# Two attentions in one program: loads and GpSimd work put at other steps, with the same arithmetic

## The chip, the core and the metric

The kernel runs on one core of a Trainium2 chip. The metric is the device time of one execution in microseconds, lower is better. Five engines work from instruction streams of their own and meet at semaphores: TensorE (PE in the profile; PEld is its weight load), VectorE (DVE), ScalarE (ACT), GpSimd (POOL) and SyncE (SP). SP computes nothing here: it issues DMA transfers, in the order of its stream, and an instruction of any stream that has to wait holds up all that stand behind it in that stream.

## The reference

Two attentions over 2048 positions of 576 features, 32 heads of 18 features each, in float32. A looks at 8 keys per query, 2 positions apart, backwards; B at all 2048 keys. Their outputs stand beside each other.

```python
# A: sliding, dilated window          S, D, H, Dh = 2048, 576, 32, 18; scale = Dh ** -0.5
q, k, v = split_heads(x @ wqkv)
idx = pos[:, None] - arange(8) * 2                 # idx < 0 is masked
logits = einsum("bhsd,bhswd->bhsw", q, k[idx]) * scale
o = einsum("bhsw,bhswd->bhsd", softmax(logits), v[idx])
a = merge_heads(o) @ wo
# B: every key
scores = einsum("bhqd,bhkd->bhqk", q, k) * scale
b = merge_heads(einsum("bhqk,bhkd->bhqd", softmax(scores), v)) @ wo
return concatenate([a, b], axis=-1)
```

## The kernel before

The program has a projection stage and a main loop.

**Projection stage** (up to 415 us). PE makes queries, keys and values, first B's and then A's. Nearly every float32 operand is split into a high and a low part, and a product is three matmuls. `stream` runs the later products two at a time on the two halves of PE's rows, and puts between them the first *maxima* of B: a matmul `bank<-ks,qs` (L159), whose 128x512 result DVE reduces to a maximum per row (L166). The stage goes by *slots*, one for each product: `at(n, f)` puts f at the n-th slot from now. The projections are written to DRAM (`dqk` for B, L468; `da` for A, L652) and read back as rows of heads. B's heads come in 8 groups g of four, and a set `qs, ks` holds one group. Three sets rotate. `second_rows`, called at a slot, makes set 1 and asks for its 12 loads (`stack_loads(1)`, L143 and L144, 288 KB each), one per slot, from POOL's own DMA queue. SP has the other transfers of the stage: the inputs of A (`raw<-xa`, `more<-xa`, L363), the weights (`raw<-wa`), and the write-backs. ACT makes the high parts and empties the banks, POOL most of the low parts (`xlo`, `olo`, `alo`).

**Main loop.** 512 *steps*, 64 per group: four blocks of 512 queries by 16 key tiles kt. A step is four score matmuls (`bank<-qs,ks`, L229), three or four maxima for later blocks (L159, L166), four exponentials on ACT (L235), and the eight matmuls `po<-e,v` (L701) of the step before, which weigh the values. Some steps also hold 27 matmuls more, a product of A's output with its output weights. Beside this goes an *agenda*: `plan` and `later` put small functions at a step number, and `due()` emits those of a step at its end. An engine keeps to the order of emission, not to the step: where nothing holds it up SP runs ahead, and POOL falls behind when it has much to do.

**The end of a block of B** (`finish`, L706). It comes at a step s that is a multiple of 16. ACT copies `po` to `o`. Then the agenda has: `den<-o`, the 4 denominators' rows out of `o` (s+1, SP, L733); a reciprocal on DVE (s+8, L734); `drec<-den` (s+9, SP) and `rec<-drec` (s+13, SP), which spread the reciprocals over partitions; *the division*, three POOL instructions `o<-o,rec`, `n<-o`, `n<-o,n` (s+18 to s+20, L737 to L739); and the store `do<-n` (s+26, SP). `rec` and `n` have one buffer each.

**A inside the main loop** (`local`). A's attention is done in 8 *parts* j of 256 positions. Part j starts at step 10 + 54j. Relative to that step: `fetch` brings queries (0), keys (1) and values (28) from `dpart`; POOL multiplies and adds for the logits `lg` (`match`, 5 to 25, nine times); DVE takes the maximum over the 8 keys in three halvings (`most`, 31 to 33, `am`, L859); POOL subtracts it (33), ACT exponentiates (35), DVE sums in three halvings (`total`, 36 to 38, `as`, L859) and inverts (`inverses`, 38 and 39, L875); POOL scales `lg` (`share`, 39, L878) and weighs the values (`weighted`, 39 to 59). The halvings are called *the trees* below. `dpart` is a copy of `da` in another layout, made before by three DRAM-to-DRAM transfers of SP (`arrange`, `dpart<-da`, L822), from 24 steps ahead of the part, and not before step 14 of the group:

```python
at = A_FROM + GAP * j - 24
at = max(at, STEPS * (at // STEPS) + 14) - A_FROM - GAP * j
```

That gives the first of the three at steps 3 (set apart for j = 0), 40, 94, 148, 206, 270, 310 and 364.

**Output weights.** `load_wo` loads a chunk of `woa` or `wob` to a tile `y` (four buffers, shared with outputs) and three steps later POOL splits it (L104, L105). A's five chunks come at steps 28, 32, ... 44, B's at 404, 408, ... 420. A's are first used at step 88, B's at 488.

Of the kernel before, what the change touches and what calls it, by code (L numbers as in the profile page):

```python
# [22 lines left out]
NG = H // 4  # L23
# [10 lines left out]
STEPS = NB * NT  # L34
# [9 lines left out]
GAP = 54  # L44

A_FROM = 10


def ap(t, *dims):

    return bass.AP(tensor=t.tensor, offset=t.offset, ap=[list(t.ap[0])] + [list(d) for d in dims])


def rows(t, *dims):

    return bass.AP(tensor=t.tensor, offset=t.offset, ap=[list(d) for d in dims])
# [3 lines left out]
def two_attentions(ctx: ExitStack, tc, xa, wa, woa, xb, wb, wob, out):  # L60
# [5 lines left out]
    nc = tc.nc  # L66
# [42 lines left out]
    step = 0  # L109
# [4 lines left out]
    def plan(start, pieces):  # L114
        for n, f in pieces:
            agenda[start + n].append(f)
# [8 lines left out]
    def make_set(pool, i):  # L125
        qs = pool.tile([128, NB, 2, 512], F32R, name=f"qs{i}")
        ks = pool.tile([128, 2, S], F32R, name=f"ks{i}")
        sets.append((qs, ks))

    def ones_loads(i):  # L130
        ks = sets[i][1].bitcast(F32)
        return [lambda r=r: load(ap(ks[64 * r + 54 : 64 * r + 56], (128, 2 * NT), (1, 128)), ap(ones, (0, 2 * NT), (1, 128)))
                for r in range(2)]
# [108 lines left out]
    def load_v(g):  # L242
        vs[g] = (work if g % 2 else maxes).tile([128, NT, 4 * 19], F32, name="v", bufs=1)
        load(vs[g], dv[g])
# [85 lines left out]
    def do_all(fs):  # L330
        for f in fs:
            f()
# [6 lines left out]
    with (tc.tile_pool(name="x", bufs=1, side="right") as xp,  # L339
# [104 lines left out]
        if True:  # L444
# [9 lines left out]
            chunks = [[(0, 0, 128)], [(0, 128, third - 128), (D, 0, 256 - third)], [(D, 256 - third, 128)]]  # L454
# [67 lines left out]
            def at(n, *fs):  # L522

                while len(todo) <= n:
                    todo.append([])
                todo[n].extend(fs)
# [24 lines left out]
            def store_values(h, v2):  # L551
                for i, v in enumerate(v2):
                    load(dv[4 * h + 2 * i : 4 * h + 2 * i + 2].rearrange("g p t c -> p g (t c)"),
                         v.rearrange("p g t h d -> p g (t h d)"))
# [22 lines left out]
            def second_rows():  # L577

                store_values(1, v2)
                kept.close()  # L580
                stack1 = ctx.enter_context(tc.tile_pool(name="stack1", bufs=1, reuse_waits="tile"))
                make_set(stack1, 1)
                do_all(ones_loads(1))
                zeros = xp.tile([128, 512], F32, name="ohi", bufs=4)
                nc.gpsimd.memset(zeros[:108, : 16 * HALO], 0.0)
                load(rows(da[0], ((HALO + S) * 16, 108), (HALO + S, 16), (1, HALO)), zeros[:108, : 16 * HALO])
                for i, f in enumerate(stack_loads(1, issue=nc.gpsimd.dma_start)):
                    at(5 + i, f)
                load_v(0)

            wa_room = ExitStack()
# [48 lines left out]
            for k in range(2, 14):  # L640
                n = 46 if k == 2 else 36 + 4 * k
# [7 lines left out]
            def leave_a(c, b, n, ps):  # L649
                o = xp.tile([128, 512], F32, name="ohi", bufs=4)  # L650
                nc.scalar.activation(o[:n], ps, AF.Copy)  # L651
                load(da[128 * c : 128 * c + n, HALO + 512 * b : HALO + 512 * b + 512], o[:n])  # L652
# [23 lines left out]
            for c, b in order:  # L676
                n = min(128, 3 * D - 128 * c)
                work_list.append(((b % 2, ws[c][0], xas[b][0], slice(0, n), every),
                                  lambda ps, n=n: ps[:n], lambda ps, c=c, b=b, n=n: leave_a(c, b, n, ps)))
# [12 lines left out]
        step = 0  # L692
# [13 lines left out]
    def finish(g, b):  # L706
        o = work.tile([128, 512], F32, name="o", bufs=2)
        if g == NG - 1 and b == NB - 1:
            return closing(b, o, work.tile([128, 512], F32, name="rec", bufs=1))
        nc.scalar.activation(o, po, AF.Copy)  # L710
        den = work.tile([128, 16], F32, name="den", bufs=2)
        rec = work.tile([128, 512], F32, name="rec", bufs=1)
        parts = []

        def room():
            if g == NG - 1 and b == 0:

                parts[:] = [ap(work.tile([128, 4, 128], F32R, name=f"at{i}", bufs=1), (1, 512)) for i in range(2)]
            else:
                n = work.tile([128, 2, 512], F32R, name="n", bufs=1)  # L720
                parts[:] = n[:, 0], n[:, 1], n
            return parts

        if g == NG - 1 and b > 0:
            return shortly(b, o, rec, *room()[:2])

        def store():
            if g < NG - 1:
                load(do[:, g, :, 512 * b : 512 * b + 512].rearrange("i p n -> p i n"), parts[2].bitcast(F32))
            else:  # L730
                plan(step, full(b, parts))

        for at, f in ((1, lambda: load(den, o[DH:128:32])),  # L733
                      (8, lambda: nc.vector.reciprocal(den, den)),  # L734
                      (9, lambda: load(drec[g, b].rearrange("i (p n) -> (i p) n", n=16), den)),
                      (13, lambda: load(rec, rows(drec[g, b], (512, 4), (0, 32), (1, 512)))),
                      (18, lambda: nc.gpsimd.tensor_mul(o, o, rec)),  # L737
                      (19, lambda: nc.gpsimd.tensor_copy(room()[0], o)),
                      (20, lambda: nc.gpsimd.tensor_sub(parts[1], o, parts[0])),  # L739
                      (26, store)):  # L740
            later(at, f)

    def shortly(b, o, rec, hi, lo):
# [45 lines left out]
    wo = {}  # L789

    producing = set()

    def load_wo(k, src, *pieces):

        raw = work.tile([128, D], F32, name="y", bufs=4)
        n = 0
        if len(pieces) == 4:
            nc.gpsimd.memset(raw, 0.0)
            n = 128
        for at, c0, m in pieces:  # L800
            load(raw[at : at + m], src[c0 : c0 + m])
            n = max(n, at + m)
        if k == "a":
            hi = work.tile([128, D], F32R, name="wohi", bufs=5)
            lo = work.tile([128, D], F32R, name="wolo", bufs=5)
        else:

            c = len(wo.get(k, []))
            hi, lo = (ap(t[:, 0, 0, :] if len(t.shape) == 4 else t[:, 0, :], (1, NB * 1024))[:, D * c : D * c + D]
                      for t in sets[(NG - 3) % 3])  # L810
        wo.setdefault(k, []).append((hi, lo))
        later(3, lambda: split_on(nc.gpsimd, hi[:n], lo[:n], raw[:n]))


    def local(j):
# [4 lines left out]
        def arrange(n):  # L820
            wide = (HALO if n else 0) + SUB
            load(rows(dparts[j][n][0, 0], (wide, D), (D * wide, 4), (1, wide)),  # L822
                 rows(da[D * n, HALO + p0 + SUB - wide :], (HALO + S, D), (SUB, 4), (1, wide)))
# [95 lines left out]
        def sums_of_a(h):  # L919
# [3 lines left out]
            if h == 0:  # L923
# [6 lines left out]
        pieces = [(0, lambda: fetch("q")), (1, lambda: fetch("k")), (28, lambda: fetch("v")), (33, lower),  # L930
                  (35, exponents), (39, share), (60, upper), (61, rest), (64, lambda: put(0)), (66, lambda: put(1))]

        pieces[:0] = [(at, lambda f=f, n=n: f(n)) for f, ats in ((most, (31, 32, 33)), (total, (36, 37, 38)),
                                                                (inverses, (38, 39))) for n, at in enumerate(ats)]
        for c in range(DH // 2):
            pieces.append((5 + 5 * c // 2, lambda c=c: match(c)))
            pieces.append((39 + 5 * c // 2, lambda c=c: weighted(c)))
        at = A_FROM + GAP * j - 24

        at = max(at, STEPS * (at // STEPS) + 14) - A_FROM - GAP * j  # L940
        for n in range(3):
            pieces.append((at + n if j else n - 7, lambda n=n: arrange(n)))
        for n, (at, ends) in enumerate(((70, (78, 80)), (81, (87, 89)))):
            pieces.append((at, lambda n=n: get(n)))
            for h in range(2):
                pieces.append((ends[h], lambda h=h: finished(h)))
                producing.add(A_FROM + GAP * j + ends[h] + 1)
            pieces.append((ends[1] + 6, lambda n=n: load(out[p0 + 128 * n : p0 + 128 * n + 128, :D], ys["a", j, n])))
# [132 lines left out]
        waiting.append(lambda: sum_of(y, t, h, olds[b]))  # L1081
        sums[t, b, h] = (y,)

    for k, src, start, chunks in (
        ("a", woa, 28, [[(0, 128 * c, 128)] for c in range(4)] + [[(64 * r, 512, 64) for r in range(2)]]),
        ("b", wob, STEPS * (NG - 2) + 20,
         [[(0, 126 * c, 126)] for c in range(4)] + [[(32 * i, 504 + DH * i, DH) for i in range(4)]]),
    ):
        plan(start, [(4 * c, lambda k=k, src=src, ch=ch: load_wo(k, src, *ch)) for c, ch in enumerate(chunks)])
    for j in range(NJ):  # L1090
        plan(A_FROM + GAP * j, local(j))
    for g in range(1, NG):
# [16 lines left out]
    total = early + rest  # L1109
# [22 lines left out]
    while step < ALL:  # L1132
        n, kt = divmod(step, NT)
        g, b = divmod(n, NB)
# [50 lines left out]
```

## Time and profile before

| | us |
|---|---|
| median of 3 runs (lowest, highest) | 1646.38 (1645.86, 1647.27) |
| the profiled execution | 1646.54 |
| its span, first to last instruction | 1644.8 |
| PE busy in the span (share) | 1633.1 (99%) |
| DVE busy | 1397.0 (85%) |
| ACT busy | 1221.9 (74%) |
| POOL busy | 959.2 (58%) |

The profiled execution has 1.74 us outside its span and lies 0.16 us above the median. The page says of itself that matmuls are pipelined and that their ends are modelled: a busy PE need not be a PE at full rate. So the loss of a step is read from the starts of matmuls. A row of the timeline gives start, duration, engine, line, operation, out<-in, shape and count; in brackets stands the idle time of the engine before it and what ended it. "SPq" is SP issuing a DMA: the time is that of the issue, not of the transfer. The rows of windows give, for each stretch, every engine's busy time with its number of instructions, the granted clock, the busy share of the DMA engines and their GB/s.

### The profile page before, as it was taken

The numbers are of one execution on the slowest core, as the hardware profiler recorded it, in microseconds if no ns is written. First come the engines' busy times: TensorE is split into PE (matmuls) and PEld (weight loads), VectorE is DVE, ScalarE is ACT, GpSimd is POOL, SyncE is SP. The second block draws the span as 40 slices with busy tenths as digits, with TensorE's granted clock in tenths as the row PEclk, the third lists the DMA queues.
The fourth block names the chain that finished last, engine by engine and source line by source line (L and its number), as shares of the span: only waits on it lengthen the run. The fifth ranks groups of instructions, "written<-read, shape, count | busy, mean of one in ns | idle before, by whom it ended". The sixth has DMA issues, their size and how long they took to land.

```text
span 1644.8 us, 33745 instructions
## 1 busy us (share of the span) xinstructions
PE 1633.1 (99%) x12906; PEld 935.0 (57%) x12906; DVE 1397.0 (85%) x2366; ACT 1221.9 (74%) x2419; POOL 959.2 (58%) x792
## 2 busy tenths in 40 slices
PE   9999999999999999999999999999999999999998
PEld 7999879998433444444344344344344344445676
DVE  5199989999899989889889899889899989888533
ACT  6314432111899998998998998998998998998554
POOL 2306642210195995994994994994995996940000
PEclk9999999999999999999999999999999999999999
DMA  8837955522515347157139325716526132033201
GB/s 252 238 113 204 257 165 140 134 87 90 95 48 100 98 120 135 54 139 143 53 93 161 82 77 130 147 65 122 134 79 117 65 107 78 21 114 123 101 37 59
DMA packets 188353, 188.22 MB, mean 114 GB/s; under 512 B 118384, under 2 KB 132208, under 8 KB 186464
## 3 DMA queue, kind: packets, MB, share of 16 engines
q1 hardware_dynamic: 183328, 174.53, 40.9%
q0 software_dynamic: 4032, 10.63, 3.0%
q8 instruction: 101, 1.65, 0.4%
q10 hardware_dynamic: 832, 0.92, 0.2%
q14 instruction: 60, 0.49, 0.1%
HBM read 113.16 MB, written 88.12 MB: 122 GB/s over the span
## 4 chain that ended last, share of the span: by engine, by line
PE 96%; DMA 2%; DVE 1%; ACT 0%; POOL 0%; issue 0%; SPq 0%; ACTq 0%; POOLq 0%; DVEq 0%
PE po L701 30%; PE bank L229 25%; PE bank L322 16%; PE bank L159 13%; PE bank L1010 7%; PE bank L259 5%; DMA den<-o 1%; DVE mx L166 1%; DMA dqk<-ohi 0%; POOL xlo L370 0%; DMA first<-xb 0%; DVE am L859 0%; SPq L363 0%; DMA out<-y 0%; PE bank L985 0%
## 5 line engine op out<-in xcount | busy, mean ns | idle before, releaser
L166 DVE TENSOR_REDUCE mx<-bank 128x1 f32<-128x512 f32 x2048 | 1288.1, 683 | 144.6 <-PE bank L159 115.8
L235 ACT ACTIVATE e<-bank 128x512 f32<-128x512 f32 x2048 | 1060.2, 613 | 94.3 <-PE bank L229 51.0
L159 PE MATMUL bank<-ks,qs 54*128 54x512 f32 x2048 | 752.7, 423 | 2.1 <-DVE mx L166 2.0
L229 PEld LDWEIGHTS bank<-qs,ks 56*128 56x128 f32 x2048 | 331.1, 186 | 454.1 <-ACT e L235 423.6
L229 PE MATMUL bank<-qs,ks 56*128 56x512 f32 x2048 | 582.0, 425 | 0.0
L701 PE MATMUL po<-e,v 128*19 128x512 f32 x4096 | 538.1, 599 | 0.0
L159 PEld LDWEIGHTS bank<-ks,qs 54*128 54x128 f32 x2048 | 340.8, 185 | 15.6 <-DVE mx L166 7.6
L841 POOL TENSOR_TENSOR pr<-aq,akv 128x1024 f32<-128x1024 f32 x72 | 158.4, 2201 | 28.1 <-DMA akv<-dpart 25.6
L701 PEld LDWEIGHTS po<-e,v 128*19 128x19 f32 x4096 | 70.6, 97 | 182.1 <-issue 171.4
L884 POOL TENSOR_TENSOR pr<-lg,akv 128x1024 f32<-128x1024 f32 x72 | 158.1, 2196 | 0.6
L845 POOL TENSOR_TENSOR pr<-pr 128x1024 f32<-128x1024 f32 x64 | 152.5, 2382 | 5.0
L651 ACT ACTIVATE ohi<-bank 128x512 f32<-128x512 f32 (+1 forms) x56 | 30.5, 595 | 148.3 <-issue 116.9
L322 PE MATMUL bank<-xlo,ahi 64*128 64x512 f32 (+1 forms) x448 | 117.9, 389 | 1.4 <-POOL xlo L370 1.4
L322 PE MATMUL bank<-xhi,alo 64*128 64x512 f32 (+1 forms) x448 | 116.1, 388 | 0.0
L322 PE MATMUL bank<-xhi,ahi 64*128 64x512 f32 (+1 forms) x448 | 113.7, 388 | 1.1 <-ACT ohi L651 1.1
L885 POOL TENSOR_TENSOR pr<-pr 128x512 f32<-128x512 f32 x72 | 92.3, 1282 | 5.6
L370 POOL TENSOR_TENSOR alo<-raw,ahi 128x512 fp32r<-128x512 f32 (+1 forms) x14 | 17.6, 1254 | 121.1 <-ACT ahi L369 86.7
L463 POOL TENSOR_TENSOR olo<-olo,ohi 128x512 fp32r<-128x512 f32 x36 | 46.1, 1294 | 63.8 <-ACT ohi L462 58.4
L737 POOL TENSOR_TENSOR o<-o,rec 128x512 f32<-128x512 f32 x29 | 37.2, 1284 | 64.3 <-DMA rec<-drec 35.4
L322 PEld LDWEIGHTS bank<-xlo,ahi 64*128 64x128 f32 (+1 forms) x448 | 67.2, 182 | 7.6 <-POOL xlo L370 2.5
L322 PEld LDWEIGHTS bank<-xhi,alo 64*128 64x128 f32 (+1 forms) x448 | 65.8, 182 | 5.3
L322 PEld LDWEIGHTS bank<-xhi,ahi 64*128 64x128 f32 (+1 forms) x448 | 63.8, 181 | 7.2 <-ACT ohi L651 1.5
(197 smaller groups left out, 1790.5 us busy)
## 6 DMA issues: line engine op xcount, KB each, us to landing
do<-n SPq DMA_DIRECT2D x28, 512.0 KB
da<-ohi SPq DMA_DIRECT2D x52, 256.0 KB
dpart<-da SPq DMA_DIRECT2D x16, 702.0 KB
akv<-dpart SPq DMA_DIRECT2D x16, 702.0 KB
out<-y SPq DMA_DIRECT2D x32, 288.0 KB
qs<-dqk SPq DMA_DIRECT2D x30, 288.0 KB
ks<-dqk SPq DMA_DIRECT2D x30, 288.0 KB
at<-dao SPq DMA_DIRECT2D x64, 128.0 KB
```

Of the source, the lines that this page charges most:

```text
L159: nc.tensor.matmul(ps, qs[at, b, p, 128 * t : 128 * t + 128], ks[at, p, 512 * k : 512 * k + 512], start=True, stop=True)
L166: nc.vector.tensor_reduce(mx[:, r, p, t, k : k + 1], ps, axis=AX.X, op=ALU.max)
L229: nc.tensor.matmul(ps, ks[at, p, 128 * kt : 128 * kt + 128], qs[at, b, p], start=True, stop=True)
L235: nc.scalar.activation(e, ps, AF.Exp, scale=SCALE)
L259: nc.tensor.matmul(ps, a, b, start=c == i == 0, stop=c == 4 and i == 1)
L322: nc.tensor.matmul(ps, a, b, start=start, stop=stop)
L701: nc.tensor.matmul(po[32 * i : 32 * i + 19], vs[g][:, kt, 19 * i : 19 * i + 19], es[i], start=kt == 0, stop=kt == NT - 1)
L841: nc.gpsimd.tensor_mul(pr, ap(st["q"][:, 2 * c], (SUB, 2), (0, W), (1, SUB)), window(st["k"], c))
L845: nc.gpsimd.tensor_add(st["pr"], st["pr"], pr)
L884: nc.gpsimd.tensor_mul(at, ap(st["lg"], (0, 2), (SUB, W), (1, SUB)), window(st["v"], c))
L885: nc.gpsimd.tensor_add(at[:, :, :4], at[:, :, :4], at[:, :, 4:])
L1010: nc.tensor.matmul(ps, a, b, start=start, stop=stop)
```

## The change

It has four parts. Each engine executes the same instructions as before, and on PE, DVE and ACT they stand in the same order. What differs is the order on POOL and SP, and the waits that follow from it.

1. `arrange` starts at steps written out in a list: 3, 36, 100, 154, 186, 250, 308, 362 for j = 0 to 7.
2. The division of a block, and its store, move later by `apart` steps: the fewest for which its three steps are none of the trees' nominal steps (`most`, `total`, `inverses` of any part). It is 6 for the block that ends at step 80, 2 at 192, 8 at 240, 4 at 352, 10 at 400, and 0 for all others.
3. The chunks of `woa` are loaded at steps 2, 4, ... 10 in place of 28, 32, ... 44, and those of `wob` at 452, 456, ... 468 in place of 404, 408, ... 420.
4. The 12 loads of set 1 are asked for 10 slots later in the projection stage.

```diff
+ARRANGED = (3, 36, 100, 154, 186, 250, 308, 362)
...
                 for i, f in enumerate(stack_loads(1, issue=nc.gpsimd.dma_start)):
-                    at(5 + i, f)
+                    at(15 + i, f)
                 load_v(0)
...
+        apart = next(k for k in range(16) if not pieces_of_a.intersection(range(step + 18 + k, step + 21 + k)))
         for at, f in ((1, lambda: load(den, o[DH:128:32])),
                       (8, lambda: nc.vector.reciprocal(den, den)),
                       (9, lambda: load(drec[g, b].rearrange("i (p n) -> (i p) n", n=16), den)),
                       (13, lambda: load(rec, rows(drec[g, b], (512, 4), (0, 32), (1, 512)))),
-                      (18, lambda: nc.gpsimd.tensor_mul(o, o, rec)),
-                      (19, lambda: nc.gpsimd.tensor_copy(room()[0], o)),
-                      (20, lambda: nc.gpsimd.tensor_sub(parts[1], o, parts[0])),
-                      (26, store)):
+                      (18 + apart, lambda: nc.gpsimd.tensor_mul(o, o, rec)),
+                      (19 + apart, lambda: nc.gpsimd.tensor_copy(room()[0], o)),
+                      (20 + apart, lambda: nc.gpsimd.tensor_sub(parts[1], o, parts[0])),
+                      (26 + apart, store)):
             later(at, f)
...
+    pieces_of_a = set()
...
-        pieces[:0] = [(at, lambda f=f, n=n: f(n)) for f, ats in ((most, (31, 32, 33)), (total, (36, 37, 38)),
-                                                                (inverses, (38, 39))) for n, at in enumerate(ats)]
+        short = [(at, lambda f=f, n=n: f(n)) for f, ats in ((most, (31, 32, 33)), (total, (36, 37, 38)),
+                                                           (inverses, (38, 39))) for n, at in enumerate(ats)]
+        pieces[:0] = short
+        pieces_of_a.update(A_FROM + GAP * j + at for at, _ in short)
...
-        at = A_FROM + GAP * j - 24
-
-        at = max(at, STEPS * (at // STEPS) + 14) - A_FROM - GAP * j
         for n in range(3):
-            pieces.append((at + n if j else n - 7, lambda n=n: arrange(n)))
+            pieces.append((ARRANGED[j] + n - A_FROM - GAP * j, lambda n=n: arrange(n)))
...
-    for k, src, start, chunks in (
-        ("a", woa, 28, [[(0, 128 * c, 128)] for c in range(4)] + [[(64 * r, 512, 64) for r in range(2)]]),
-        ("b", wob, STEPS * (NG - 2) + 20,
+    for k, src, start, apart, chunks in (
+        ("a", woa, 2, 2, [[(0, 128 * c, 128)] for c in range(4)] + [[(64 * r, 512, 64) for r in range(2)]]),
+        ("b", wob, STEPS * (NG - 1) + 4, 4,
          [[(0, 126 * c, 126)] for c in range(4)] + [[(32 * i, 504 + DH * i, DH) for i in range(4)]]),
     ):
-        plan(start, [(4 * c, lambda k=k, src=src, ch=ch: load_wo(k, src, *ch)) for c, ch in enumerate(chunks)])
+        plan(start, [(apart * c, lambda k=k, src=src, ch=ch: load_wo(k, src, *ch)) for c, ch in enumerate(chunks)])
```

## The prediction

> **What bounds the kernel.** I read the page's engines first, then the timeline of PE in the main loop, those of DVE, ACT and SP, the instructions of L859, POOL's timeline, and the windows of the projection stage.
>
> ```profile
> PE 1633.1 (99%) x12906; PEld 935.0 (57%) x12906; DVE 1397.0 (85%) x2366; ACT 1221.9 (74%) x2419; POOL 959.2 (58%) x792
> ```
>
> PE never rests by this, so what can be won shows only in the distance between starts. These are the last matmuls of successive steps:
>
> ```profile
> 892.84 1.05 PE L701 MATMUL po<-e,v 128*19 128x512 f32 x8
> 894.95 1.05 PE L701 MATMUL po<-e,v 128*19 128x512 f32 x8
> 897.69 1.05 PE L701 MATMUL po<-e,v 128*19 128x512 f32 x8
> 899.91 1.05 PE L701 MATMUL po<-e,v 128*19 128x512 f32 x8
> ...
> 908.35 1.05 PE L701 MATMUL po<-e,v 128*19 128x512 f32 x8
> 912.46 1.30 PE L701 MATMUL po<-e,v 128*19 128x512 f32 x8
> 915.70 1.45 PE L701 MATMUL po<-e,v 128*19 128x512 f32 x8
> 918.21 1.05 PE L701 MATMUL po<-e,v 128*19 128x512 f32 x8
> ```
>
> An undisturbed step takes 2.11 us (892.84 to 894.95). ACT and DVE stand close behind:
>
> ```profile
> 890.21 8.33 ACT L235 ACTIVATE e<-bank 128x512 f32<-128x512 f32 x16
> ```
> ```profile
> 903.56 1.89 DVE L166 TENSOR_REDUCE mx<-bank 128x1 f32<-128x512 f32 x3 [0.21 <-PE bank L159]
> 909.99 0.25 DVE L734 RECIPROCAL den<-den 128x16 f32<-128x16 f32 x1 [2.44 <-DMA den<-o]
> ```
>
> Sixteen exponentials are four steps of ACT, 2.08 us a step. DVE spends 1.89 of a step on maxima and has 0.21 to spare. So PE's order, ACT and DVE bound together: anything over 0.21 us that DVE does or waits for in a step is paid by PE. The change leaves the orders of PE, DVE and ACT as they were, so there is nothing to win but such waits.
>
> **Part 1, the copies of A.** The three steps from 908.35 to 918.21 take 9.86 us where 3 x 2.11 = 6.33 would do: 3.53 lost, at the reciprocal that waited. SP's queue says for what:
>
> ```profile
> 883.59 12.82 SPq L822 DMA_DIRECT2D dpart<-da  x3
> 896.50 5.74 SPq L733 DMA_DIRECT2D den<-o  x1
> ```
>
> Issuing three `dpart` copies held SP for 12.82 us; `den<-o` (step 209) stood behind those of steps 206 to 208, began at 896.50 and landed when the reciprocal (step 216) began, at 909.99. From the first copy to the landing it took 26.4 us. The ten steps that it had are 21.1 us. The new starts are 36, 100, 154, 186, 250, 308 and 362. After 154, 186, 250 and 362 the next reciprocals (168, 200, 264, 376) are 14 steps off, 29.5 us, 3.1 more than the worst stretch; the others stand behind that boundary's `den` and are further from the next. So the 3.53 go. Late next is `drec` or `rec` behind the copies, which only holds POOL's division, and POOL runs some steps behind its agenda anyway. Bounds: 0, if another `den` or `rec` becomes as late, and -3.53. I take -3.5.
>
> **Part 2, the division off the trees.** The halvings of A by operation (columns: shortest, median and longest in ns):
>
> ```profile
> L859 DVE TENSOR_TENSOR am<-am x16: 207/276/1017, 511.2 to 1378.7; 128x128 f32<-128x128 f32 x8, 128x64 f32<-128x64 f32 x8
> L859 DVE TENSOR_TENSOR as<-as x16: 207/280/1007, 521.7 to 1393.9; 128x128 f32<-128x128 f32 x8, 128x64 f32<-128x64 f32 x8
> L859 DVE TENSOR_TENSOR am<-lg x8: 414/416/1368, 508.8 to 1373.8; 128x256 f32<-128x256 f32 x8
> L859 DVE TENSOR_TENSOR as<-lg x8: 412/415/728, 519.6 to 1389.5; 128x256 f32<-128x256 f32 x8
> ```
>
> Undisturbed they are 0.41 (256 columns), 0.28 (128) and 0.21 (64). The long ones coincide with a POOL operation:
>
> ```profile
> 893.72 1.29 POOL L737 TENSOR_TENSOR o<-o,rec 128x512 f32<-128x512 f32 x1 [7.29 <-DMA rec<-drec]
> ```
> ```profile
> 894.08 1.01 DVE L859 TENSOR_TENSOR as<-as 128x64 f32<-128x64 f32 x1
> ...
> 1002.30 1.37 DVE L859 TENSOR_TENSOR am<-lg 128x256 f32<-128x256 f32 x1
> ...
> 1266.86 0.75 DVE L859 TENSOR_TENSOR as<-as 128x128 f32<-128x128 f32 x1
> ...
> 1375.99 0.95 DVE L859 TENSOR_TENSOR am<-am 128x128 f32<-128x128 f32 x1
> ...
> 1378.66 1.02 DVE L859 TENSOR_TENSOR am<-am 128x64 f32<-128x64 f32 x1
> ```
>
> POOL's multiply runs to 895.01, and the halving that began inside it ends at 895.09, 0.80 late. PE's steps after it are 2.74 and 2.22: 0.63 + 0.11 = 0.74 lost for 0.80. The other overruns are 0.96, 0.47, 0.67, 0.81, and 0.32 for the longest `as<-lg`. Less the 0.21 of slack each, they cost 0.75 + 0.26 + 0.46 + 0.60 + 0.11 = 2.2; at the rate of the first, 0.92 x 3.23 = 3.0. I take 2.2. All these trees have a division at their steps, which `apart` takes off: -0.74 - 2.2 = -2.9. Bounds: 0 and -3.7.
>
> Where do the divisions go? Their price, and where POOL has room:
>
> ```profile
> 633.97 1.29 POOL L737 TENSOR_TENSOR o<-o,rec 128x512 f32<-128x512 f32 x1
> ...
> 636.01 1.28 POOL L739 TENSOR_TENSOR n<-o,n 128x512 fp32r<-128x512 f32 x1
> ...
> 650.30 1.28 POOL L878 TENSOR_TENSOR lg<-lg,as 128x512 f32<-128x512 f32 x1 [13.01 <-ACT e L235]
> ...
> 746.50 1.29 POOL L848 TENSOR_TENSOR lg<-pr 128x512 f32<-128x512 f32 x1
> 748.02 1.28 POOL L737 TENSOR_TENSOR o<-o,rec 128x512 f32<-128x512 f32 x1 [0.23 <-DMA at<-dao]
> ...
> 995.47 1.29 POOL L848 TENSOR_TENSOR lg<-pr 128x512 f32<-128x512 f32 x1
> ...
> 1121.00 1.28 POOL L848 TENSOR_TENSOR lg<-pr 128x512 f32<-128x512 f32 x1
> ```
> ```profile
> 751.66 0.41 DVE L859 TENSOR_TENSOR am<-lg 128x256 f32<-128x256 f32 x1
> ...
> 1126.64 0.42 DVE L859 TENSOR_TENSOR am<-lg 128x256 f32<-128x256 f32 x1
> ```
>
> A division takes POOL 3.3 us (633.97 to 637.29). It leaves the wait before `share` (13.01 us idle at 650.30), and stands between the products of `weighted` and the next part's `match`, where POOL has no idle time. So the next `lg` comes 3.3 later. In part 2 `lg` was ready at 747.79 for a tree at 751.66: 3.9 - 3.3 = 0.6 is left, but the unmoved division at 748.02 shifts to 751.3 and now covers the first halving with its multiply and the second with its last step. Two collisions at 0.74 would be 1.5; the multiply starts some tenths ahead of the first halving, which shortens that one, and I take 0.9. In part 5, 4.4 - 3.3 = 1.1 is left, and the division behind `lg` grazes the tree: 0.3. In part 4 `lg` ended 5.5 ahead of 1002.30, of which the 3.5 won by PE eat most; nothing is added. Part 7 gets one division and loses two weight splits. Together +1.2; bounds 0 and, with two collisions in each of parts 2 and 5, 4 x 0.74 = 3.0.
>
> The Trainium skill, *SBUF — State Buffer*, "Who interferes with whom", says that a VectorE operation with two SBUF inputs and a GpSimd operation that reads SBUF exclude each other, and that issue order decides which blocks. Where the halving is issued first, POOL would be the one to wait: by that the 1.2 would be 0 and the time 1.2 lower. The rows above show only the case where POOL was first.
>
> **Part 3, output weights.** Cost 0, and the cover is POOL's rest:
>
> ```profile
> 448.22 4.37 POOL L841 TENSOR_TENSOR pr<-aq,akv 128x1024 f32<-128x1024 f32 x2 [25.64 <-DMA akv<-dpart]
> ```
> ```profile
> 1448.00:1490.00 42.00, 42.00 (x328) 19.17 (x328) 37.08 (x62) 37.79 (x75) 8.16 (x9) 1.00 0.35 112
> ```
>
> `woa`'s splits fall into the 25.64 us before POOL's first product; their loads share SP with part 0's `aq` and `akv`, which may come some us later, ahead of a first tree at 508.8. `wob` goes to the stretch around 1448 to 1490, where POOL works 8.16 of 42 us and the DMA engines 0.35. If that cover were gone (loads of the next head group late by one issue of 5 us, as 896.50 shows), it would cost up to 5; I see no such row.
>
> **Part 4, second rows.** The twelve loads, issued by POOL at one per slot, ended at 190.19; ten slots later they would go out from about 187 to 226, an estimate from the places of the next products in the trace (the last window below is where that stretch ends):
>
> ```profile
> 190.19 0.61 POOL L143 DMA_DIRECT2D ks<-dqk  x1
> ```
> ```profile
> 171.39 0.63 ACT L369 ACTIVATE xhi<-raw 128x512 fp32r<-128x512 f32 x1 [8.61 <-DMA raw<-xa]
> ```
> ```profile
> 170.00:180.00 10.00, 9.57 (x83) 8.00 (x81) 9.50 (x16) 5.73 (x10) 7.65 (x9) 1.00 0.99 304
> ...
> 210.00:220.00 10.00, 9.57 (x84) 7.50 (x80) 9.24 (x15) 1.82 (x3) 6.50 (x7) 1.00 0.89 269
> 220.00:230.00 10.00, 7.97 (x60) 5.57 (x62) 6.30 (x11) 4.50 (x8) 5.10 (x5) 1.00 0.62 185
> ```
>
> ACT waited 8.61 us for A's input while those loads were under way and the DMA engines full (share 0.99). PE missed 0.43 there and 0.43 + 2.03 at 210 to 230. If A's inputs now come early and the chain runs ahead, up to 2.9 are won; if the moved loads stand before the later inputs, a wait like 8.61 is paid in full. The load leaves a full stretch for one at 0.89 and 0.62, with room but not for all of it: between gain and loss I take 0.
>
> **Sum.** -3.5 - 0.7 - 2.2 + 1.2 + 0 + 0 = -5.2 against the profiled execution's 1646.5: 1641.3. The median lies 0.16 lower, so 1641.1 as a median. A change within 0.2% (3.3 us, 1643.1 to 1649.7) is about what a measurement can't tell from none.
>
> **Rivals.**
>
> *Other side: second rows delay A's inputs.* The twelve loads at 187 to 226 stand in the DMA engines before `raw<-xa` and `more<-xa`; PE waits for the product. For it: 8.61 at 171.39, and a share of 0.89 without them. Against: 0.62 at 220, and PE missed only 0.43 at the time of the 8.61. Price 8.6: 1641.1 + 8.6 = 1649.7. It undoes the gain from 5.2 us on, and makes the kernel slower beyond the measurement from 8.6. Chance 0.16. The Trainium skill, *DMA: Bandwidth & Descriptors*, "Issuing engines are not separate DMA queues", says that transfers interleave on the same 16 engines whoever issues them, so POOL's own queue is no shelter; the 0.99 share agrees.
>
> *POOL late.* The moved divisions make `lg` late or collide in parts 2, 4 and 5: 3 x 2 x 0.74 = 4.4 in place of 1.2: 1644.3. For it: POOL's chain without gaps; against: 13 us of idle at each `share`. Chance 0.17.
>
> *Part 1 does not do what it says.* Another `den` waits behind copies, or `rec` comes so late that POOL's chain holds a tree; the 3.5 return: 1644.6. For it: 12.82 us of SP per trio wherever it stands; against: 3.1 us of margin. Chance 0.11.
>
> **Numbers.** My forecast has 0.56, with a range of its own of 1637 (second rows win their 2.9, no new collision) to 1643. The range 1636.5 to 1648.5 leaves out the larger half of the first rival and the tails. Faster: 0.57; the second and third rivals and the smaller part of the first are within 0.2%: 0.30; slower 0.13.
>
> **What would show it.** Part 1: no reciprocal of `den` with an idle time by `den<-o`, and steps of 2.11 at the former 908. Part 2: the longest of L859 near 0.28 to 0.42, except `am` in parts 2 and 5. Part 3: the same starts of `am<-lg` in part 0 and no wait of PE after 1448. Part 4: ACT's idle time for `raw` and `more` at 187 to 230, and PE's busy time in those windows. The prediction is wrong if PE's windows there fall by several us, or if halvings run over in new places.

## The result: slower by 0.37%, and the profile after

| | before | changed |
|---|---|---|
| median, us (6 runs each) | 1646.99 | 1653.6 |
| lowest to highest | 1645.86 to 1649.76 | 1652.49 to 1654.52 |
| span of the profiled execution | 1644.8 | 1652.7 |

The ratio is 1.0037, with a 95% interval of 1.0027 to 1.0048. The forecast was 1641.1 us, with a range of 1636.5 to 1648.5.

The gains came in the size that was worked out. PE's last matmuls of the steps that the late reciprocal had stretched, in the timeline of the changed kernel:

```profile
906.65 1.05 PE L703 MATMUL po<-e,v 128*19 128x512 f32 x8
908.76 1.05 PE L703 MATMUL po<-e,v 128*19 128x512 f32 x8
910.87 1.05 PE L703 MATMUL po<-e,v 128*19 128x512 f32 x8
912.97 1.05 PE L703 MATMUL po<-e,v 128*19 128x512 f32 x8
915.08 1.05 PE L703 MATMUL po<-e,v 128*19 128x512 f32 x8
```

They stand 2.11 apart. The halvings of A (now line 864; shortest, median, longest in ns):

```profile
L864 DVE TENSOR_TENSOR am<-am x16: 208/246/620, 516.6 to 1380.2; 128x128 f32<-128x128 f32 x8, 128x64 f32<-128x64 f32 x8
L864 DVE TENSOR_TENSOR as<-as x16: 215/248/283, 527.1 to 1395.0; 128x128 f32<-128x128 f32 x8, 128x64 f32<-128x64 f32 x8
L864 DVE TENSOR_TENSOR am<-lg x8: 415/416/1108, 514.3 to 1376.0; 128x256 f32<-128x256 f32 x8
L864 DVE TENSOR_TENSOR as<-lg x8: 415/416/417, 525.0 to 1390.6; 128x256 f32<-128x256 f32 x8
```

The sums (`as`) have no long one left; of the maxima two are long, 1.11 and 0.62. They are those of part 2, where the division that wasn't moved now covers the tree, as forecast. Part 5's first one, at 1129.28, takes 0.58: it is grazed, as forecast too.

What the forecast did not have are two places where PE stands still. The waits of PE by what ended them (total us, times, longest):

```profile
PE bank L324 <- ACT ohi L653: 6.9, 1, 6.9
PE po L703 <- ACT o L712: 4.0, 1, 4.0
```

*The projection stage.* ACT before, then ACT and PE in the changed kernel, and the windows that answer to those shown of before (busy times in the order PE, PEld, DVE, ACT, POOL):

```profile
216.63 0.63 ACT L405 ACTIVATE ohi<-raw 64x512 fp32r<-64x512 f32 x1 [6.75 <-DMA dqk<-ohi]
```
```profile
222.21 0.63 ACT L407 ACTIVATE ohi<-raw 64x512 fp32r<-64x512 f32 x1 [9.67 <-DMA dqk<-ohi]
```
```profile
226.42 0.80 PE L324 MATMUL bank<-xhi,ahi 64*128 64x512 f32 x2 [6.88 <-ACT ohi L653]
```
```profile
170.00:180.00 10.00, 10.00 (x90) 9.99 (x88) 9.95 (x17) 8.15 (x15) 8.10 (x9) 1.00 0.81 270
...
210.00:220.00 10.00, 9.55 (x84) 9.09 (x80) 9.20 (x15) 1.26 (x2) 5.14 (x7) 1.00 1.04 227
220.00:230.00 10.00, 3.58 (x16) 2.83 (x18) 1.50 (x3) 5.56 (x10) 6.11 (x6) 0.71 0.92 253
```

The stretch at 170 got air (share 0.81, PE without a gap), and the one at 210 to 230 filled up: PE missed 0.45 + 6.42 there, where it had missed 2.46, and its clock fell, to a mean of 0.71 in the last row. The chain says what ACT's buffer waited for, first before, then changed:

```profile
211.30 5.22 DMA dqk<-ohi
```
```profile
212.47 9.63 DMA dqk<-ohi
```

One and the same write-back of B's projection takes 5.22 and 9.63 us. It begins 1.17 us later than before and lasts 4.41 us longer; together that is the 5.58 us by which ACT's `ohi` is later. The first weighing of the main loop shows what is left of it, before and changed:

```profile
422.57 1.05 PE L701 MATMUL po<-e,v 128*19 128x512 f32 x8
```
```profile
428.04 1.05 PE L703 MATMUL po<-e,v 128*19 128x512 f32 x8
```

The main loop starts 5.47 us later.

*The end of block 432.* POOL, ACT and PE in the changed kernel:

```profile
1403.93 1.28 POOL L741 TENSOR_TENSOR o<-o,rec 128x512 f32<-128x512 f32 x1
...
1410.69 1.26 POOL L743 TENSOR_TENSOR n<-o,n 128x512 fp32r<-128x512 f32 x1
```
```profile
1411.99 0.60 ACT L712 ACTIVATE o<-po 128x512 f32<-128x512 f32 x1 [4.09 <-POOL n L743]
```
```profile
1406.43 1.05 PE L703 MATMUL po<-e,v 128*19 128x512 f32 x8
1412.64 1.92 PE L703 MATMUL po<-e,v 128*19 128x512 f32 x8 [4.02 <-ACT o L712]
1416.49 1.91 PE L703 MATMUL po<-e,v 128*19 128x512 f32 x8
1419.65 1.05 PE L703 MATMUL po<-e,v 128*19 128x512 f32 x8
```

`o` has two buffers, so the block that ends at step 432 takes that of block 400. Its division, moved by 10, stands at steps 428 to 430 among the products of `weighted`, and its last instruction ended at 1411.95. That instruction began some 7 us, over three steps, after the matmuls of its step 430 had ended. ACT could not copy `po`, and PE could not begin the next block. Three steps took 13.22 us (1406.43 to 1419.65) where 6.33 would do: 6.9 lost, of which 4.0 are the wait. The rest is the clock: these matmuls take 1.9 us in place of 1.05. In windows of 2 us (the column before the last two is the granted clock):

```profile
1410.00:1412.00 2.00, 0.00 (x0) 0.00 (x0) 0.00 (x0) 0.01 (x1) 1.92 (x4) 0.99 0.00 0
1412.00:1414.00 2.00, 1.36 (x8) 0.16 (x8) 0.00 (x0) 2.00 (x5) 1.92 (x3) 0.50 0.01 2
...
1416.00:1418.00 2.00, 2.00 (x11) 0.16 (x8) 1.28 (x3) 1.38 (x3) 1.89 (x3) 0.50 0.02 3
...
1420.00:1422.00 2.00, 2.00 (x19) 0.84 (x15) 1.77 (x4) 1.95 (x5) 1.84 (x3) 1.00 0.00 0
```

A third, smaller wait came at step 206:

```profile
887.42 0.40 PE L1014 MATMUL bank<-wohi,at 64*128 64x288 f32 x2 [1.19 <-DMA at<-dao]
```

### The profile page after: what moved, and what is told of

Read it like the earlier page. It is cut to its first block, busy times and chain, and to the rows that moved or that the text cites. A ratio compares the mean times of both kernels' runs of the same rounds, so it can differ in the third digit from the quotient of the medians.

```text
span 1652.7 us, 33736 instructions
## 1 busy us (share of the span) xinstructions
PE 1633.2 (99%) x12906; PEld 961.5 (58%) x12906; DVE 1394.6 (84%) x2366; ACT 1222.0 (74%) x2419; POOL 960.4 (58%) x792
## 4 chain that ended last, share of the span: by engine, by line
PE 94%; DMA 3%; POOL 1%; DVE 1%; ACT 0%; SPq 0%; issue 0%; ACTq 0%; POOLq 0%; DVEq 0%
PE po L703 30%; PE bank L231 25%; PE bank L324 14%; PE bank L161 13%; PE bank L1014 7%; PE bank L261 4%; DMA dqk<-ohi 1%; DMA at<-dao 1%; DMA dqk<-olo 1%; DVE mx L168 0%; DMA raw<-xa 0%; DMA first<-wb 0%; POOL pr L889 0%; POOL pr L890 0%; DMA out<-y 0%
## 5 line engine op out<-in xcount | busy, mean ns | idle before, releaser
L883 POOL TENSOR_TENSOR lg<-lg,as 128x512 f32<-128x512 f32 x8 | 10.2, 1281 | 112.4 <-DVE as L880 58.0
```

## The experiments

The first four put one part of the change into the kernel before; the others take parts of the changed kernel back. Beside them the kernel before had medians of 1649.95, 1649.67 and 1649.38 us (single runs from 1645 to 1657), so ratios are compared, not times. Each run also has one traced execution. Traces differ too: the first weighing begins at 420.9 to 425.1 us in the eight that have the loads of set 1 at their old slots. So a trace is used for the place and the cause of a loss, the medians for its size.

**Part 4 alone.**

```diff
-                    at(5 + i, f)
+                    at(15 + i, f)
```

> The kernel before with part 4 alone (the 12 loads of set 1 ten slots later). Theory: the moved loads by themselves fill the DMA engines at 187 to 230 us and hold back the write-backs of B's projection and with them ACT and PE; the main loop then starts 5.5 us later and the time is 1646.5 + 5.5 = 1652, with a wait of PE of about 7 us near 219 to 226. Rival, that the wait in the changed kernel comes of another part: within 1 us of 1646.5 and no such wait.

Measured: 1.0028 (1.0014 to 1.0042), 4.6 us. PE's wait is there:

```profile
225.69 0.80 PE L322 MATMUL bank<-xhi,ahi 64*128 64x512 f32 x2 [6.34 <-ACT ohi L651]
```

The moved loads make it alone. The traces of all runs sort by them. In the three with the loads ten slots later and issued by POOL (this one, the changed kernel, and block 400 moved by 4) the write-back `dqk<-ohi` took 7.93 to 9.63 us, ACT waited 9.49 to 9.71 us for it, and the first weighing began at 427.5 to 428.1. In the eight with the loads at their old slots the write-back took 4.04 to 5.71 us and ACT waited 4.81 to 6.95. PE's wait sorts less well: with the loads at their old slots it is at most 1.5 us in six traces, but 3.3 with part 1 alone and 4.2 with both edits taken back (below). So some of the 5.47 us between the first two traces is spread; the medians give 4.6.

**Part 1 alone.**

```diff
-            pieces.append((at + n if j else n - 7, lambda n=n: arrange(n)))
+            pieces.append((ARRANGED[j] + n - A_FROM - GAP * j, lambda n=n: arrange(n)))
```

> The kernel before with part 1 alone (the written-out starts of the copies of A). Theory: the 3.5 us at steps 218 and 219 go, a wait of PE of about 1.2 us for at<-dao comes at step 206, and the collisions of division and tree stay but for the one at 894, whose division waited for rec: 1646.5 - 3.5 - 0.7 + 1.4 = 1643.7. Rival, that the copies also delay what ACT and PE waited for in the changed kernel at 220 and 1408: 1648 or more.

Measured: 1.0004 (0.9991 to 1.0016), so neither. The reciprocal's 3.5 us are gone, and come back elsewhere: DVE now waits for POOL's `lg` in part 4 and, 1.99 us, in part 7, and PE for `at<-dao` at 206 and at 260. These are DVE in part 4, and POOL 100 us before it:

```profile
1003.71 0.42 DVE L861 TENSOR_TENSOR am<-lg 128x256 f32<-128x256 f32 x1 [2.02 <-POOL lg L850]
```
```profile
903.30 1.28 POOL L739 TENSOR_TENSOR o<-o,rec 128x512 f32<-128x512 f32 x1 [13.40 <-ACT e L237]
```

Before, this `lg` was 5.5 us ahead of its tree. Two things make it late now. The stall at step 218 had given POOL 3.5 us, and those are gone. And `rec<-drec`, behind the copies of 186 to 188, is issued at 892.61, where it was 882.95 before: some 6 us later against PE's steps. The row of POOL names ACT, but the division begins 10.7 us after that issue, much as before (893.72 after 882.95, where the row names `rec<-drec`), so it is `rec` that it waited for. `share` stands behind it and comes 4 us later against PE's steps. In the changed kernel this division (block 192) is two steps later, `share` goes ahead of it, and that tree is in time.

**Part 2 alone.** (The copies, weights and second rows as before.)

```diff
+        apart = next(k for k in range(16) if not pieces_of_a.intersection(range(step + 18 + k, step + 21 + k)))
...
-                      (18, lambda: nc.gpsimd.tensor_mul(o, o, rec)),
+                      (18 + apart, lambda: nc.gpsimd.tensor_mul(o, o, rec)),
```

> The kernel before with part 2 alone (divisions moved off the trees). Theory: the division of block 400, now at steps 428 to 430, ends after step 432, where ACT wants the same o buffer again, so PE stands about 4 us near 1410 and its clock falls for some steps: +6.7; part 2's halvings are hit, +0.6; the tree collisions go, -2.2 to -2.9: 1646.5 + 4.8 = 1651.3. Rival, that this wait needs the other parts too (copies or weights): no wait of ACT for n there and about 1644.7.

Measured: 1.0091 (1.0072 to 1.011), 15 us: more than expected. ACT's wait for `n` is there without the other parts, and so are two trees for which `lg` is late; this is part 5:

```profile
1424.17 0.60 ACT L712 ACTIVATE o<-po 128x512 f32<-128x512 f32 x1 [4.11 <-POOL n L743]
```
```profile
1131.65 1.47 DVE L864 TENSOR_TENSOR am<-lg 128x256 f32<-128x256 f32 x1 [2.61 <-POOL lg L853]
```

POOL had stood still for a buffer there, too. The store of block 240, moved by 8 to step 274, stood in SP's queue behind the copies, which without part 1 are still at 270 to 272, and the next block's division had to wait for the one buffer `n`:

```profile
1061.77 0.61 POOL L742 CAST n<-o 128x512 fp32r<-128x512 f32 x1 [4.33 <-DMA do<-n]
```

Part 7's tree is 2.72 late; there the weight splits, which part 3 takes away, still stand in POOL's chain. And the late `den` of step 218 costs 6.6 us in place of 3.5, since DVE waited 4.03 us for it and PE's clock fell. So the parts are not additive: alone, parts 4, 1, 2 and (next) 3 give +0.28, +0.04, +0.91 and -0.07%, which is +1.16% in sum, and the changed kernel with all four has +0.37%.

**Part 3 alone.**

```diff
-        ("a", woa, 28, ...
-        ("b", wob, STEPS * (NG - 2) + 20,
+        ("a", woa, 2, 2, ...
+        ("b", wob, STEPS * (NG - 1) + 4, 4,
```

> The kernel before with part 3 alone (loads of the output weights moved). Theory: nothing waits for the weights; the splits leave POOL's chain at part 7's tree, so at most the 1.0 us lost at step 422 goes: 1645.5 to 1646.5. Rival, that weights or head rows come late: a wait of PE after step 452 or before step 40, and 1648 or more.

Measured: 0.9993 (0.998 to 1.0005). The matmuls of step 422, 1.04 us late before, are in time now; nothing waits for weights. Without the splits in its chain POOL ends part 7's `lg` at about 1369.4 and does block 400's division, unmoved, until 1372.74; the tree begins behind it, at 1373.91, with halvings of 0.42, 0.29 and 0.22.

**Part 4 undone.**

```diff
-                    at(15 + i, f)
+                    at(5 + i, f)
```

> The changed kernel with part 4 undone. Theory: 1653.6 - 5.5 = 1648.1, with the wait near 1410 still there. Rival, that the earlier weights or copies take part in the wait near 220: it stays in part, and the time is above 1650.

Measured: 0.9995 (0.9984 to 1.0006); against the changed kernel's 1.0037 that is 0.42%, some 7 us, with 5.5 expected. ACT's wait for `n` at the end of block 432 stays, at 4.09 us.

**Block 400 moved by 4, not 10.**

```diff
+        apart = {400: 4}.get(step, apart)
```

> The changed kernel with the division of block 400 moved by 4 steps instead of 10 (steps 422 to 424, into POOL's idle time before share). Theory: ACT's wait for n at the end of block 432 and the fall of the clock behind it go, 6.7 us, and the tree of part 7 is not hit, since the division runs between its two trees: 1646.9. Rival, that POOL is late there whatever the division does: the wait stays, 1653; or the tree is hit again: 1647.7.

Measured: 0.9994 (0.9982 to 1.0006), again 0.43% under the changed kernel. POOL does the division in the idle time behind the maxima, and ACT copies in time:

```profile
1383.34 1.29 POOL L871 TENSOR_TENSOR lg<-lg,am 128x512 f32<-128x512 f32 x1 [5.53 <-DVE am L865]
1384.60 1.29 POOL L742 TENSOR_TENSOR o<-o,rec 128x512 f32<-128x512 f32 x1
```
```profile
1410.48 0.63 ACT L712 ACTIVATE o<-po 128x512 f32<-128x512 f32 x1
```

**Both taken back.** (The two edits above together.)

> The changed kernel with part 4 undone and block 400's division moved by 4 instead of 10: only the two edits that cost most are taken back. Theory (the two losses are separate and add): 1653.6 - 5.5 - 6.7 = 1641.4 on the scale of the changed kernel, about 0.3% under the kernel before; left over are a wait for at<-dao at step 206 (1 to 3 us) and part 2's halvings (0.6). Rival, that one of the waits only hid the other's cause: 1646 or more.

Measured: 0.9972 (0.9959 to 0.9984). That is 0.65% under the changed kernel, where the single edits gave 0.42 and 0.43: within the intervals they add, and without them the change is a gain of 0.28%. The rival, that one wait hid the other's cause, falls.

**Few bytes at the new slots.**

```diff
-                for i, f in enumerate(stack_loads(1, issue=nc.gpsimd.dma_start)):
+                for i, f in enumerate(stack_loads(1, (2, DH - 2), issue=nc.gpsimd.dma_start)):
+                    at(5 + i, f)
+                for i, f in enumerate(stack_loads(1, (0, 2), issue=nc.gpsimd.dma_start)):
                     at(15 + i, f)
```

> The changed kernel with each of the 12 loads of set 1 cut in two: 2 of its 18 rows at the new slots, 16 at the old ones. POOL issues as often at the new slots, with a ninth of the bytes. If the bytes in the DMA engines made the wait near 220, it is gone: 1653.6 - 5.5 = 1648.1, perhaps a little more for twelve further issues of POOL at the old slots. If POOL's issue time in the chain of xlo made it, it stays: 1653.

Measured: 1.0034 (1.0019 to 1.0049), which doesn't decide by itself. The place does: PE's longest wait at 220 shrinks from 6.88 to 2.97, while a new stall comes at 170, where POOL has twelve more issues and the DMA engines are full again. And the write-back `dqk<-ohi` takes 4.70 us, as with the loads at their old slots, though POOL issues as often at the new ones.

```profile
224.85 0.50 PE L324 MATMUL bank<-xhi,ahi 64*128 64x512 f32 x2 [2.97 <-ACT ohi L655]
```
```profile
170.00:180.00 10.00, 8.40 (x70) 7.02 (x68) 8.13 (x14) 5.85 (x10) 7.13 (x9) 1.00 1.02 245
```

**The same loads from SP.**

```diff
-                for i, f in enumerate(stack_loads(1, issue=nc.gpsimd.dma_start)):
+                for i, f in enumerate(stack_loads(1)):
```

> The changed kernel with the 12 moved loads of set 1 issued by SP at the same new slots, not by POOL. The bytes and their place stay, POOL's issue time and its descriptors go, and SP's queue gets 12 more issues before the last write-backs of B. If the bytes in the DMA engines hold back the write-backs, ACT's wait for dqk<-ohi near 212 to 222 and PE's stay, 1653 or more; if POOL's part made them, they go back to the 6.7 us of the kernel before with PE idle about 2.5 us, and the time is 1648.

Measured: 1.0048 (1.0029 to 1.0068). POOL has no part in these loads any more, and a wait of this size is there:

```profile
225.19 0.80 PE L324 MATMUL bank<-xhi,ahi 64*128 64x512 f32 x2 [5.77 <-ACT ohi L653]
```

So POOL's issue time isn't needed for such a wait. But this one comes by another way: in the chain `more<-xa`, an input of A, takes 8.12 us, SP issues the write-back that ACT waits for only at 219.52, among loads in its own queue, and it then takes 2.38 us. It is the run with few bytes that shows that the bytes lengthen the write-back; this one doesn't.

**Five slots later, not ten.**

```diff
+                    at(10 + i, f)
```

> The changed kernel with the loads of set 1 moved by 5 slots, not 10. Theory: the DMA engines have room neither in the old stretch nor in the new one; the wait near 220 shrinks with what of the loads still falls before it: PE idle between 2.5 and 7 us at 210 to 230, 1649 to 1653. Rival, that the last few loads alone decide: still about 7 us and 1653.

Measured: 1.0014 (1.0 to 1.0028), in between, as expected. PE's wait of 4.49 us doesn't decide, since 4.2 was seen with no load moved; the write-back took 5.28 us, which is as with the old slots.

**A version with four mends.**

```diff
-ARRANGED = (3, 36, 100, 154, 186, 250, 308, 362)
+ARRANGED = (3, 36, 100, 154, 210, 250, 308, 362)
...
+        apart = {400: 4, 80: 0}.get(step, apart)
...
-                    at(15 + i, f)
+                    at(5 + i, f)
```

> The changed kernel with part 4 undone, block 400 moved by 4, block 80 not moved, and the copies for part 4 from step 210 instead of 186. Theory: the losses of 5.5, 6.7, 0.6 and 1.4 go and the gains of 6.4 stay: 1653.6 - 14.2 = 1639.4. Rival, that copies at 210 make the next den or rec late, or that A's queries come late: 2 to 4 us more.

Measured: 0.9944 (0.9928 to 0.9961), 1641.08 against 1649.67. It beats both kernels: 0.56% under the one before. In its trace the steps around 206, 218 and 432 take their usual time, and no halving is longer than 0.45 us.

**The same with the copies at 186.**

> The version with all four mends, but the copies for part 4 again from step 186. Theory: copies at 186 to 188 hold SP's at<-dao of step 199 back, so PE waits at step 206: 1 to 3 us more than with the copies at 210, a time of 1640.5 to 1642 where that version would have 1639.4 (0.1 to 0.2% between them). Rival, that the wait came of the moved division of block 80: none at 206 and no difference.

Measured: 0.996 (0.9945 to 0.9975). The intervals of the two overlap, so the difference of times isn't shown; its place is. With 186, PE waits at step 206, and with 210 no such row is there:

```profile
879.63 0.40 PE L1015 MATMUL bank<-wohi,at 64*128 64x288 f32 x2 [1.08 <-DMA at<-dao]
```

The other rival, block 80's division, falls: it isn't moved in either.

## Why the prediction was wrong

**The gains were right in size, and one was booked under the wrong part.** By the length of each step, from PE's starts against the median of steps of its kind, PE won 0.72 at 212 and 213, 3.50 at 218 and 219, 0.73 at 259, 0.44 at 373 and 1.04 at 422, together 6.4 us; the forecast had 3.5 + 0.74 + 2.2. But the 1.04 stood under part 2, as "all these trees have a division at their steps". Of the two long halvings there, the one at 1378.66 ran beside a split of weights (`ks<-y,qs`, L105, 1378.16 to 1379.59), and part 3 alone wins the 1.04. So with part 3 alone block 400's division needed no move; whether it needs one in the changed kernel, where `lg` ends 0.83 us ahead of that tree, no run shows.

**The new collisions were nearly right.** Part 2 was to cost 0.9 and part 5 0.3. Part 2 cost 0.62, and some 0.4 are scattered over steps 260, 266, 267 and 313, of which only 0.1 at 313 are part 5's.

**The step that failed first: the price of a moved division was only what it does to the next `lg`.** "It leaves the wait before `share` ... and stands between the products of `weighted`" counted POOL's time ahead of a tree, and nothing of who waits for the division itself. It reads `o`, which has two buffers, so a block has 32 steps until its buffer is wanted again; the working never names that limit. Moved by 10, block 400's last step was at nominal 430 of 432, and POOL ran over three steps behind. That it does so was written down, as a reason why lateness of `rec` is harmless; here the same lag is what broke it. Measured: 6.9 us. No rival had it.

**The second: part 4 was taken as 0.** The rows shown held both ends, -2.9 and +8.6, and the middle was taken. The first rival was the right mechanism, for the most part at another transfer. A's input `raw<-xa` does stand in the changed kernel's chain (6.17 us), and the write-back behind it begins 1.17 us later; but 4.41 us are the write-back itself, `dqk<-ohi`, which holds ACT's `ohi` buffer and was already ACT's longest wait of that stretch before (the 6.75 us above; the prediction didn't show that row). Measured: 5.5 us between the two traces, 4.6 between medians with part 4 alone, for a forecast of 0 and a rival of 8.6. What the Trainium skill says beside that rival (*DMA: Bandwidth & Descriptors*, "Issuing engines are not separate DMA queues") held here: the transfer delayed was SP's, the loads were POOL's.

**Part 1's rival came true elsewhere.** No `den` was late, but `at<-dao`, behind the copies of 186 to 188: 1.39 us at step 206. With part 1 alone its other half came true as well: `rec` was so late that POOL's chain held a tree, by 2.02 us. That "POOL runs some steps behind its agenda anyway" hides lateness is the same mistake.

**The sum.** -6.4 + 1.0 + 1.4 + 6.7 (the three steps, less what they lost before) + 5.5 = +8.2, against 7.9 between the spans. The 1.4 at step 206 is one execution's: in the eight other traces with copies at 186 it cost 1.3 to 3.8. Part 3 cost nothing, as forecast, but won the 1.04 us named above.

## What to carry to other kernels

When an instruction is moved later, follow each buffer that it reads to the next writer of that buffer, and count the distance against the engine's lag, not against the agenda; here two steps were left and the lag was over three. Where transfers leave a full stretch for another one, the transfer to watch is the one that already ends the longest wait there. And a stall that is removed takes away time that a late engine had used, so parts of a change are not to be judged one by one: parts 1, 2 and 3 give +0.88% in sum when each stands alone, and -0.05% together (part 4 undone).

## What the runs showed of the hardware

A short stop of PE can cost more than its length. After 4.02 us the granted clock stood at 0.50 for about 6 us, which added 2.9 us. Much shorter stops can do it too. In the run with both edits taken back, the wait at step 206 was 2.07 us, and in the 8 us ahead of it PE had been busy without a gap:

```profile
885.14 0.40 PE L1015 MATMUL bank<-wohi,at 64*128 64x288 f32 x2 [2.07 <-DMA at<-dao]
```
```profile
886.00:888.00 2.00, 2.00 (x21) 1.71 (x17) 1.37 (x2) 0.30 (x1) 0.00 (x0) 0.65 0.92 301
888.00:890.00 2.00, 2.00 (x10) 0.16 (x8) 1.05 (x2) 0.71 (x2) 0.00 (x0) 0.50 0.78 209
```

That step and the next lost 3.83 us; the one with 1.19 us of wait in the changed kernel kept its clock at 1.00 and lost 1.39. The Trainium skill, *TensorE: Matmul & The Clock Gate*, "HAM oscillation — how this bites in real kernels", gives as a rule no idle gaps of PE above about 3.4 us. The measurement decides: a gap of 2.07 was enough here. Nor do the gaps at this step sort by length: after 1.53 us (block 400 moved by 4) the clock fell to 0.50, after 1.56 us (part 4 undone) it stayed at 1.00; what decides between them these runs don't show. The 3.53 us that the late reciprocal cost before were in part such a fall, too, after a gap of PE of 1.01 us:

```profile
914.00:916.00 2.00, 2.00 (x11) 1.01 (x13) 1.44 (x3) 1.48 (x4) 1.84 (x4) 0.50 0.98 335
```

The matmuls of 1.30 and 1.45 us that the prediction shows there had been a sign of it.
